# Two attention and gated-MLP layers in one kernel: key weights on GpSimd's queue, warm-ups on a cleared strip, new tables for the order

## The chip, the cores and the metric

The kernel runs on one core of a Trainium2 chip. The metric is the device time of one execution in microseconds, as the median of several runs. Times inside an execution come from one profiled execution, and are counted from its first instruction.

## The reference

The input `x` has 2048 rows of 512 numbers in bf16. Two layers with the same weights follow each other. Each layer adds two blocks to `x`, and each block works on the layer norm of `x`.

```python
def _A_ref(x, wqkv, wo):              # H = 32 heads of 16, window W = 256
    qkv = (x @ wqkv).reshape(B, S, 3, H, Dh)          # then to q, k, v by head
    scores = einsum("bhqd,bhkd->bhqk", q, k) * Dh ** -0.5
    mask = (i - j >= 0) & (i - j < W)                 # a causal sliding window
    p = softmax(where(mask, scores, -1e9))
    return einsum("bhqk,bhkd->bhqd", p, v).reshape(B, S, D) @ wo

def _B_ref(x, w_gate, w_up, w_down):  # F = 1792
    h = sigmoid(x @ w_gate) * (x @ w_up)
    return h @ w_down

for layer in range(2):
    x = x + _A_ref(layernorm(x), A_wqkv, A_wo)
    x = x + _B_ref(layernorm(x), B_w_gate, B_w_up, B_w_down)
```

## The kernel before

All weights and all of `x` stay in SBUF. The 2048 rows are 16 tiles of 128 rows; four tiles are a group, for which queries, keys and values are projected. `layer_norm` makes one tile's normalised rows: statistics on DVE (`stats`, L589 to L592), one over the root on POOL (`root`, L598 and L599), the scaling into `xn` on DVE (`apply`, L617), and then the transposed copy `xnT`. The first tiles are transposed by PE (L638) and copied out by ACT or DVE (L666, L668); the later ones go by a transposing DMA on SP's queue (L656), two tiles at a time.

PE's matmuls are the projections (queries L703, keys L734, values L770), the scores (L1029, L1040, L1050), the values times the probabilities (L1109), the output projection (L893), gate and up of the MLP (L798, called GLU in the code), and down (L862). Scores and values run with the array split, four small matmuls side by side; the others use it whole. ACT takes the exponential of a whole score buffer, `Sps`, at once (L1082, 128 x 2048 elements). One such step is a visit. There is one score buffer, so the next scores wait for the exponential ahead of them. A layer has 77 visits, the kernel 154. There are 64 blocks of values, two for each tile in each layer. After the values come a transposition, the normalisation and a second transposition (by PE for tiles 0 and 1, by SP's queue for the others), then the output projection, and after that the second layer norm, gate and up, and down.

`GLU` says how many tiles share one pass over gate and up: a pass over one, two or four tiles has matmuls of 128, 256 or 512 columns. A pass over four tiles can begin when `xnT` of all four is there. `TAIL` cuts the last tile's down product into 384 and 128 columns.

No order of instructions is written by hand. `Plan` is a small model of the chip that runs while the kernel is built. It keeps a clock for each engine, durations for each kind of work (such as `EXP_NS`, `SWITCH`, or the number that `scores` returns), and the times at which DMAs land. Whenever an engine is free in this model, the ready task with the lowest priority number is emitted on it; PE's next piece of work is chosen in `pick` and `choose`. So the order on every queue follows from the tables: `PRIO` and `LATE_PRIO` for the tasks of ACT, DVE, POOL and SP, `RANK` and `LATE_RANK` for PE, `SLACK` and `LATE_SLACK` for what is added to a DMA's landing, `OPT` for variants, and `PACE`. `PACE` holds the smallest time between the starts of two visits: entry 0 in layer 0, entry 1 in layer 1, entry 2 in the first 12 visits, entry 3 from there to visit 23. The LATE tables hold after visit 23. On the chip the order is fixed, and each engine waits by semaphores for what it needs.

Where the model has nothing for PE, `keep_warm` (L1292) emits four matmuls of 128 columns whose result nobody reads. Their operand is the identity `ident`, which POOL makes first thing in `constants`. POOL also writes `nhalf`, the exponent of `root`, and clears the halves of `Vl` and `Vh` (L534) that the copies from `Vaug` leave alone. `Vl` and `Vh` are filled by DMAs on SP's queue (L1314).

`loads` issues the inputs on the queues of SP and ACT: tiles 0 to 3 of `x` in halves, then the weights of the keys, of the queries (each in two transfers of 256 KB, one on each queue), and of the values, then the other inputs. `has_wq["k"]` is the event that a key projection waits for in the model.

Of the kernel before, what the change touches and what calls it, by code (L numbers as in the profile page):

```python
# [12 lines left out]
P = 128  # L13
# [43 lines left out]
def pool_ns(n):  # L57
# [2 lines left out]

EXP_NS = 1880
TAIL = (384, 128)
GLU = [[[1] * 4 + [4], [1] * 4 + [2] * 2, [1] * 6 + [2], [1] * 8, [2] * 4, [1] * 2 + [2] * 3, [2] * 2 + [4]], [[4] * 3 + [2, 1, 1], [4] * 3 + [2, 2], [4] * 4]]
PACE = [2682, 3207, 1600, 2511, 23.52]
EARLY = 12
FILL = 800
OVERLAP = {"ACT": 114, "DVE": 83, "POOL": 45, "SP": 0}
# [1 line left out]
EXTRA = {"ACT": 40, "DVE": 10, "POOL": 30, "SP": 0}  # L69
PE_LATENCY = 180  # L70
COLD = 5200
SWITCH = 96
LAND = 1230
RATE = ((3300, 330.0), (5300, 160.0), (1e9, 345.0))
FIRST = 1100
# [3 lines left out]
FETCH = (1200, 2300)  # L79


PRIO = dict(st_x0=7.13, ap_x0=2.72, xt_x0=3.36, st_x1=-0.44, ap_x1=1.86, xt_x1=6.58, st_x=18.87, ap_x=6.56,
    xt_x=2.0, st_p=7.13, ap_p=4.46, xt_p=0.81, st_g=2.23, ap_g=1.32, xt_g=6.14, st_g0=5.97, ap_g0=3.21,
    xt_g0=1.33, tp=5.75, tp_g=-0.06, q=4.0, q0=5.51, q1=4.74, k=1.95, k0=-0.89, k1=-1.49, s=-1.15, s0=5.46,
    s1=3.28, v=0.28, v0=5.43, v1=14.72, vv=5.53, exp=3.64, exp0=4.71, m0=4.61, m00=-0.56, e0=1.11, e00=1.28,
    e1=7.21, e10=6.56, m2=0.64, m20=3.6, th=5.12, mu=-0.12, dn=1.29, add=-0.27, add0=1.8, out=-2.4, mv=5.8,
    mv0=6.23, oq=-2.27, oq0=-0.14, no=4.71, no0=2.61, on=5.93, on0=0.59, vc=9.2, vc0=-0.87)
OPT = dict(gu='SP', g1=1, bk=3, bq=2, wide=0, r0=2, g0=1, g2=1, x0=1, eps=1, hold=0, own=1, ck=0, cq=2,
    turn=2)
SLACK = dict(xt=1208, oq=843, on=211, vc=1208)  # L90
RANK = dict(tp=-1.708, o=-2, lead=14.747, far=7.411, v=9.3, g=1.778, d=1.823, feed=11.672, x3=21097, wd=474,
    go=364)
LATE_PRIO = dict(st_p=-0.04, ap_p=7.96, xt_p=-0.99, st_x=1.07, ap_x=4.81, xt_x=-1.16, st_g=1.75, ap_g=1.19,
    xt_g=2.76, q=3.84, k=4.33, s=4.05, v=0.61, exp=1.12, m0=4.62, e0=2.79, e1=4.39, m2=5.49, th=1.65, mu=2.51,
    dn=2.1, add=0.69, out=0.45, mv=3.49, oq=0.77, no=6.44, on=2.16, vc=0.22)
LATE_SLACK = dict(xt=489, oq=1327, on=2346, vc=897)
LATE_RANK = dict(tp=-2, o=1.576, lead=9.722, far=6.159, v=1.796, g=1.769, d=3.896, feed=7.551, go=1418)

# [268 lines left out]
class Net:  # L369
# [74 lines left out]
    def loads(self, A_x, wqkv, wo, w_gate, w_up, w_down):  # L444
        nc, pl = self.nc, self.pl
        wq_src = wqkv.rearrange("(k p) m -> p k m", p=P)
        wo_src = wo.rearrange("(k p) m -> p k m", p=P)
        wd_src = w_down.rearrange("(c p) m -> p c m", p=P)
        wg_src = w_gate.rearrange("(k p) f -> p k f", p=P)
        wu_src = w_up.rearrange("(k p) f -> p k f", p=P)  # L450
        self.has_x, self.has_wq = {}, {}

        def load(dst, src, nbytes, after=0, prio=2, queue="SP", ns=650, row=2 * D):
            q = {"SP": nc.sync, "ACT": nc.scalar}[queue]
            return pl.dma(ns, nbytes, lambda: q.dma_start(out=dst, in_=src), (), prio, after, queue, bulk=(queue, row)).done

        def load_x(dst, tiles, n, prio=2, queues=("SP", "SP"), after=0):
            done, parts = Event(), []
            for z in range(2):
                src = A_x[0].rearrange("(t z k) d -> z k t d", z=2, k=HP)[z][:, tiles, :]  # L460
                parts.append(load(dst[z:P:2], src, n * HP * D * 2, after, prio, queues[z], 780))
            when_all(parts, done.fire)
            return done

        def x_group(g, after=0):
            h = slice(g * NBG, (g + 1) * NBG)
            ev = load_x(self.xsb[:, h, :], h, NBG, after=after)
            for t in range(g * NBG, (g + 1) * NBG):
                self.has_x[t] = ev

        def both(parts):
            done = Event()
            when_all(parts, done.fire)
            return done

        for t, n in {1: ((0, 1), (1, 1), (2, 2)), 2: ((0, 2), (2, 2)), 3: ((0, 1), (1, 3))}[OPT["x0"]]:
            ev = load_x(self.xsb[:, t:t + n, :], slice(t, t + n), n, 0, ("SP", "ACT"))
            for i in range(t, t + n):
                self.has_x[i] = ev
        if OPT["wide"]:  # L480
            self.has_wq["q"] = self.has_wq["k"] = both([
                load(self.wq[:, k:k + 2, 0:2 * D], wq_src[:, k:k + 2, 0:2 * D], 4 * P * D * 2, prio=0, queue=q, row=4 * D)
                for k, q in ((0, "ACT"), (2, "SP"))])
        else:
            for w in "kq":
                h = slice("qk".index(w) * D, ("qk".index(w) + 1) * D)
                self.has_wq[w] = both([load(self.wq[:, k:k + 2, h], wq_src[:, k:k + 2, h], 2 * P * D * 2, prio=0, queue=q)
                                       for k, q in ((0, "ACT"), (2, "SP"))])
        self.has_wq["v"] = load(self.wq[:, :, 2 * D:3 * D], wq_src[:, :, 2 * D:3 * D], D * D * 2, prio=0, queue="ACT")
        x_group(1)  # L490
        self.has_wo = load(self.wot[:], wo_src, D * D * 2)
        x_group(2)
        gu = [load(w[:, k:k + 2], src[:, k:k + 2], D * F, prio=0 if OPT["gu"] == "ACT" else 2, queue=OPT["gu"], row=2 * F)
              for w, src in ((self.wg, wg_src), (self.wu, wu_src)) for k in (0, 2)]
        self.has_gu = both(gu)
        at = RANK["x3"]
        x_group(3, at)
        parts = []
        for i in range(0, FC, 2):
            h = slice(i, i + 2)  # L500
            parts.append(load(self.wd[:, h, :], wd_src[:, h, :], 2 * P * D * 2, after=at + 2 * RANK["wd"] * i))
        self.has_wd = both(parts)

    def constants(self):
        nc = self.nc
        nc.gpsimd.memset(self.nhalf[:], -0.5)
        nc.gpsimd.memset(self.ident[:], 0.0)
        nc.gpsimd.affine_select(out=self.ident[:], in_=self.ident[:], compare_op=ALU.not_equal, fill=1.0,
                                base=0, pattern=[[-1, P]], channel_multiplier=1)
        for i in range(2):  # L510
            self.ones(i, nc.vector)
        nc.vector.memset(self.rms[0][:], 0.0)
        for m in range(4):
            nc.vector.memset(self.rms[0][32 * m:32 * m + 16, :], 1.0)
        nc.vector.tensor_scalar(out=self.rms[1][:], in0=self.rms[0][:], scalar1=-1.0, scalar2=1.0,
                                op0=ALU.mult, op1=ALU.add)
        for i in range(2):
            self.zeros(0, i)
        self.pl.free["POOL"] = 3000.0
        self.pl.free["SP"] = self.pl.free["ACT"] = 750.0  # L520
        self.pl.at(750.0)
        self.pl.at(1500.0)
        self.pl.free["DVE"] = 3600.0
        self.pl.at(3600.0)
# [11 lines left out]
    def later_constants(self):  # L536
        nc, pl = self.nc, self.pl
# [10 lines left out]
        def mask2(e):  # L548
            for z in range(2):
# [7 lines left out]
            nc.vector.tensor_scalar(out=self.maske[:, 1], in0=self.maske[:, 0], scalar1=-1.0, scalar2=1.0,  # L557
                                    op0=ALU.mult, op1=ALU.add)

        for i in range(2):  # L560
            self.vzero[i] = pl.task({"POOL": 800}, lambda e, i=i: self.zeros(1, i), first, prio=8, port=True).done
        for i in range(2, VP):
# [439 lines left out]
    def scores(self, L, t, kind, i):  # L1002
# [5 lines left out]
        if kind == "A":  # L1008
# [21 lines left out]
                                         rhs=self.qT[32 * m:32 * m + 32, i, q0:q0 + n * HP],  # L1030
                                         start=True, stop=True, tile_position=(32 * m, 0))
            runs = cut
            return pl.count(8 * len(runs)) or 220
        if kind == "R":
            zs = range(2 if t + 2 < NT else 1)
            for z in zs:
                for cq in range(NCQ):
                    q0, o = ((L * NT + t) * 2 + 5 * z) % (QG * TGW // HP) * HP, (z * NCQ + cq) * HP
                    for m in range(4):
# [1 line left out]
                                         lhsT=kTp[32 * m:32 * m + 32, cq, tt].rearrange("p e k -> p (e k)")[:, z:2 * P:2],  # L1041
                                         rhs=self.qT[32 * m:32 * m + 32, cq, q0:q0 + HP],
                                         start=True, stop=True, tile_position=(32 * m, 0))
            return pl.count(16 * len(zs)) or 122 * len(zs)
        for cq in range(NCQ):
            for e in range(2):
                o = (2 * cq + e) * HP
                q0 = ((L * NT + t) * 2 + 1) % (QG * TGW // HP) * HP
                for m in range(4):
                    nc.tensor.matmul(self.sps[:, m, o:o + HP], lhsT=kTp[32 * m:32 * m + 32, cq, tt, e, :],  # L1050
                                     rhs=self.qT[32 * m:32 * m + 32, cq, q0:q0 + HP],
                                     start=True, stop=True, tile_position=(32 * m, 0))
        return pl.count(32) or 230

    def exp(self, L, t, kind, i):
        nc = self.nc
# [27 lines left out]
    def values(self, L, t, half, bank):  # L1084
# [7 lines left out]
        for col in range(4):  # L1092
# [10 lines left out]
            for k, (where, Va, p) in enumerate(parts):  # L1103
# [6 lines left out]
                                     stop=k == len(parts) - 1 or t == 0, tile_position=(0, 32 * g))  # L1110
                n += 0.5 + 0.5 * (k == 0 and t > 0)
                pl.count(4)
        return n * 56

    def after_values(self, L, t, half, bank, done):
        nc, pl = self.nc, self.pl
# [171 lines left out]
    def keep_warm(self, bank):  # L1288

        nc, pl = self.nc, self.pl  # L1290
        for i in range(4):
            nc.tensor.matmul(self.banks[bank][:, 0:P], lhsT=self.ident[:], rhs=self.ident[:], start=True, stop=True)  # L1292
        pl.count(4)
        pl.matmul("d", 4 * 56)

# [7 lines left out]
    def half_values(self):  # L1303
# [18 lines left out]
        for z in range(2):  # L1322
            some = pairs if z == 0 else [k for k in pairs if k[1] + 2 < NT]
            for i, (L, t) in enumerate(some):
                V = self.Vaug[(L * NT + t) // 2 % VP]
                deps = [self.v_ready[L, t], self.v_ready[L, t + 1]]
                if z and i < 2:
                    deps.append(self.vzero[i])
                if i >= 2:
                    old = some[i - 2]  # L1330
                    deps += both(old[0], old[1] + 1 + 2 * z)
# [81 lines left out]
    def go(self, *srcs):  # L1413
# [26 lines left out]
        self.slot = 0  # L1440
        self.last_s = -1e9
        self.pv_list = [k + (h,) for k in LT for h in range(2)]
        self.constants()
        self.loads(*srcs)
        self.streams = [[], [], [], [], []]
        self.roots, self.pairs, self.vones, self.vzero = {}, {}, {}, {}
        self.applied = [Event() for _ in range(NBG)]
        for t in range(NBG):
            self.layer_norm(("p", 0, 0), t, [self.has_x[t]])
# [72 lines left out]
```

The softmax here doesn't subtract the row's maximum and nothing guards it: scores larger than these inputs give would overflow.

## Time and profile before

| what | value |
|---|---|
| median of 3 runs | 541.65 us (540.52 to 541.98) |
| span of the profiled execution | 539.6 us |
| PE busy | 531.1 us, 98% |
| DVE busy | 420.5 us, 78% |
| ACT busy | 382.3 us, 71% |
| POOL busy | 43.4 us, 8% |
| PE's first matmul starts, last one ends | 1.45 us, 536.35 us |
| first and last exponential start | 13.94 us, 471.26 us |
| warm-up matmuls | 64, all before 9.5 us |

No time of the profiled execution other than its span is given. PE's busy time counts from a matmul's start to its modelled end; neighbours overlap, so the mean duration of a row is longer than the distance between two starts. PEld is the loading of the stationary operand, beside the matmuls. The chain of work that ended last starts at the last instruction and goes back, at each step, to what released it.

### The profile page before, as it was taken

To read this page: it belongs to the slowest core of one execution; us is meant where nothing else is said; L and a number is where in the kernel's file an instruction comes from. 1 tells how busy PE (TensorE), PEld (TensorE's weight loads), DVE (VectorE), ACT (ScalarE), POOL (GpSimd) and SP (SyncE) were. 2 spreads that over 40 slices of the span, in tenths; PEclk is the share of its full clock that TensorE was granted. 3 is DMA by queue.
4 is the path that set the end of the run, shared out by engine and by line. 5 is a ranking of instruction groups with operands and counts; after the bars stand their busy time and mean duration, and the time that the engine had idled before them with its cause. 6 is when DMAs were issued, how large, how long until landed. Compare 5 with 4: busy or idle time off the path is not lost.

```text
span 539.6 us, 21359 instructions
## 1 busy us (share of the span) xinstructions
PE 531.1 (98%) x9658; PEld 293.0 (54%) x9658; DVE 420.5 (78%) x844; ACT 382.3 (71%) x380; POOL 43.4 (8%) x99
## 2 busy tenths in 40 slices
PE   8999999999999999999999999999999999999997
PEld 8446755855767444544444444544444444455873
DVE  6999999789878997798977789778677785674442
ACT  4989989878888687776778767787667866540330
POOL 5301110001000110101100010101000000000000
PEclk9999999999999999999999999999999999999999
DMA  8890334232421323143110622117211241132001
GB/s 260 317 227 15 43 72 57 50 61 63 72 52 33 72 51 60 36 101 59 32 35 14 105 51 47 38 42 108 54 45 28 60 72 50 24 70 58 2 11 39
DMA packets 95067, 36.23 MB, mean 67 GB/s; under 512 B 78336, under 2 KB 93952, under 8 KB 94976
## 3 DMA queue, kind: packets, MB, share of 16 engines
q1 hardware_dynamic: 93600, 33.56, 29.9%
q8 instruction: 75, 1.23, 1.0%
q10 hardware_dynamic: 1376, 1.31, 0.8%
q14 instruction: 16, 0.13, 0.1%
HBM read 9.70 MB, written 2.10 MB: 22 GB/s over the span
## 4 chain that ended last, share of the span: by engine, by line
PE 89%; DVE 5%; ACT 2%; DMA 1%; issue 1%; POOL 0%; SPq 0%; ACTq 0%; POOLq 0%
PE bank L798 37%; PE bank L862 18%; PE bank L1109 9%; PE Sps L1029 7%; PE bank L893 5%; PE bank L734 4%; PE bank L770 3%; PE bank L703 3%; PE Sps L1040 2%; ACT PTring L1082 1%; DMA wq<-in_A_wqkv_dram 1%; DVE kTp L749 1%; DVE st L589 1%; DVE PTring L960 1%; DVE edge L960 1%
## 5 line engine op out<-in xcount | busy, mean ns | idle before, releaser
L1082 ACT ACTIVATE PTring<-Sps 128x2048 bf16<-128x2048 f32 (+1 forms) x122 | 226.0, 1852 | 63.2 <-PE Sps L1029 59.2
L798 PE MATMUL bank<-xnT,wu 128*128 128x512 bf16 (+2 forms) x728 | 128.2, 297 | 0.0
L798 PE MATMUL bank<-xnT,wg 128*128 128x512 bf16 (+2 forms) x728 | 128.2, 298 | 0.0
L862 PE MATMUL bank<-wd,hT 128*128 128x512 bf16 (+2 forms) x462 | 109.9, 373 | 0.0
L824 DVE SCALAR_TENSOR_TENSOR hT<-hT,bank 128x256 bf16<-128x256 bf16 (+1 forms) x154 | 80.8, 537 | 34.0 <-ACT hT L816 21.2
L816 ACT ACTIVATE hT<-bank 128x256 bf16<-128x256 f32 (+1 forms) x154 | 71.1, 482 | 48.5 <-PE bank L798 47.8
L798 PEld LDWEIGHTS <-wg 128*128 128x128 bf16 x728 | 60.7, 98 | 36.7 <-issue 2.3
L798 PEld LDWEIGHTS <-wu 128*128 128x128 bf16 x728 | 61.4, 98 | 34.5 <-issue 2.5
L1082 ACT ACTIVATE edge<-Sps 128x2048 bf16<-128x2048 f32 (+1 forms) x32 | 56.6, 1770 | 17.3 <-PE Sps L1040 17.3
L862 PEld LDWEIGHTS <-hT 128*128 128x128 bf16 x462 | 43.0, 98 | 46.4 <-issue 2.2
L668 DVE CAST OTs<-bank 128x512 bf16<-128x512 f32 x59 | 43.0, 729 | 21.5 <-PE bank L1109 21.1
L960 DVE TENSOR_TENSOR PTring<-PTring,mask 128x1024 bf16<-128x1024 bf16 x64 | 43.7, 684 | 12.3 <-ACT PTring L1082 12.1
L1109 PE MATMUL bank<-PTring,Vaug 128*32 128x64 bf16 (+1 forms) x2880 | 52.0, 203 | 0.0
L1109 PEld LDWEIGHTS <-Vaug 128*32 128x32 bf16 x2880 | 44.0, 97 | 12.0 <-issue 10.4
L1029 PE MATMUL Sps<-qT,kTp 32*128 32x256 bf16 (+3 forms) x1216 | 47.4, 248 | 1.2 <-ACT PTring L1082 1.1
L598 POOL TENSOR_SCALAR st<-st 128x2 f32<-128x2 f32 (+1 forms) x33 | 10.7, 325 | 443.6 <-DVE st L590 443.6
L589 DVE BATCH_NORM_STATS2 st<-xsb 128x6 f32<-128x512 bf16 x64 | 43.9, 686 | 1.7 <-DMA xsb<-in_A_x_dram 1.2
L1109 PE MATMUL bank<-edge,Vl 128*32 128x64 bf16 x1024 | 44.4, 193 | 0.1
L960 DVE TENSOR_TENSOR edge<-edge,maske 128x1024 bf16<-128x1024 bf16 x60 | 40.3, 682 | 3.4 <-ACT edge L1082 3.3
L1029 PEld LDWEIGHTS <-kTp 32*128 32x128 bf16 x1216 | 18.2, 92 | 45.4 <-issue 43.5
L1109 PE MATMUL bank<-edge,Vh 128*32 128x64 bf16 x896 | 40.8, 193 | 0.0
L960 DVE TENSOR_TENSOR PTring<-PTring,maskn 128x1024 bf16<-128x1024 bf16 x56 | 38.2, 682 | 0.0
(73 smaller groups left out, 522.0 us busy)
## 6 DMA issues: line engine op xcount, KB each, us to landing
Vl<-Vaug SPq DMA_DIRECT2D x32, 68.0 KB, 2.4
out_dram<-xsb SPq DMA_DIRECT2D x15, 128.0 KB, 2.1
Vh<-Vaug SPq DMA_DIRECT2D x28, 68.0 KB, 2.5
wg<-in_B_w_gate_dram SPq DMA_DIRECT2D x2, 896.0 KB, 9.7
wu<-in_B_w_up_dram SPq DMA_DIRECT2D x2, 896.0 KB
wd<-in_B_w_down_dram SPq DMA_DIRECT2D x7, 256.0 KB, 5.3
xsb<-in_A_x_dram SPq DMA_DIRECT2D x6, 256.0 KB, 7.4
wq<-in_A_wqkv_dram ACTq DMA_DIRECT2D x2, 256.0 KB, 4.5
```

The lines of the kernel that those rows point to most:

```text
L589: nc.vector.bn_stats(out=st[:, 0:6], in_=self.xsb[:, t, :])
L668: self.nc.vector.tensor_copy(out=out, in_=in_)
L734: return [(mm_ns(w), lambda kt=kt, o=o: nc.tensor.matmul(self.banks[bank][:, o:o + w], lhsT=self.wq[:, kt, D + cq * P:D + cq * P + P], rhs ...
L798: return [(mm_ns(w), lambda i=i, j=j, fc=fc, wt=wt, kt=kt: self.nc.tensor.matmul(pt[:, i, j, :], lhsT=wt[:, kt, fc * P:(fc + 1) * P], rhs= ...
L816: self.nc.scalar.activation(out=self.hT[:, ch[0] * GW:ch[0] * GW + size], in_=pt, func=AF.Tanh, scale=0.5)
L824: self.nc.vector.scalar_tensor_tensor(out=h, in0=h, scalar=1.0, in1=pt, op0=ALU.add, op1=ALU.mult)
L862: nc.tensor.matmul(self.banks[bank][:, 0:w], lhsT=self.hT[:, at:at + P], rhs=self.wd[:, fc, d], start=fc == 0, stop=fc == FC - 1)
L893: return [(mm_ns(D), lambda c=c: nc.tensor.matmul(self.banks[bank][:], lhsT=b[0][:, c, :], rhs=self.wot[:, c, :], start=c == 0, stop=c == ...
L960: done = pl.task({"DVE": dve_bf_ns(1024)}, lambda e: nc.vector.tensor_tensor(out=r, in0=r, in1=m.to_broadcast([P, 16, HP]), op=ALU.mult), ...
L1029: nc.tensor.matmul(self.sps[:, m, o:o + n * HP], lhsT=kTp[32 * m:32 * m + 32, i, tt, e, :], rhs=self.qT[32 * m:32 * m + 32, i, q0:q0 + n * ...
L1082: nc.scalar.activation(out=out, in_=src, func=AF.Exp, scale=scale)
L1109: nc.tensor.matmul(o, lhsT=Va[:, c0:c0 + 32], rhs=p(h), start=k == 0 or t == 0, stop=k == len(parts) - 1 or t == 0, tile_position=(0, 32 * g))
```

## The change

The key weights' two transfers leave the queues of SP and ACT and are issued on GpSimd's queue, ahead of all of POOL's memsets. In the model their arrival is the constant `KEYS_NS`. The clearing of the `Vl` halves moves from `constants` to tasks (`lzero`) that are released by the root of tile 3, and the copies into `Vl` wait for it. The warm-up matmuls read the first 128 columns of `hT`, which DVE clears first thing, in place of `ident`. `hT` is otherwise the buffer of gate times up, and is first written for that much later. Several costs of the model are set higher: `SWITCH`, the scores (220 to 234, 122 to 126, 230 to 244) and the values (56 to 59.3). All tables get new numbers; `hold=1` lets the statistics of tiles 2 and 3 wait for the scaling of the tile two before, and `r1` is read nowhere. Layer 0's first half is cut into single tiles and pairs in another order; layer 1 goes from three groups of 4 tiles and two pairs to four groups of 4.

```diff
-GLU = [[[1] * 4 + [4], [1] * 4 + [2] * 2, ...], [[4] * 3 + [2, 1, 1], [4] * 3 + [2, 2], [4] * 4]]
-PACE = [2682, 3207, 1600, 2511, 23.52]
+GLU = [[..., [1, 1, 2, 1, 1, 2], [1, 1, 1, 1, 2, 2]], [[4, 4, 4, 4], [4, 4, 4, 4], [4, 4, 4, 4]]]
+PACE = [2682, 3226.51, 1293.37, 0, 23.52]
...
-SWITCH = 96
+KEYS_NS = 6600
+SWITCH = 100
...
-OPT = dict(gu='SP', g1=1, bk=3, bq=2, wide=0, r0=2, g0=1, g2=1, x0=1, eps=1, hold=0, own=1, ck=0, cq=2,
-    turn=2)
-SLACK = dict(xt=1208, oq=843, on=211, vc=1208)
+OPT = dict(gu='SP', g1=1, bk=3, bq=2, wide=0, r0=2, g0=5, g2=1, x0=1, eps=1, hold=1, own=1, ck=0, cq=2,
+    turn=2, r1=1)
+SLACK = dict(xt=3684, oq=1183, on=0, vc=1448)
...
-            for w in "kq":
+            for w in "q":
...
-    def constants(self):
+    def constants(self, wqkv):
         nc = self.nc
+        nc.vector.memset(self.hT[:, 0:P], 0.0)
+        src = wqkv.rearrange("(k p) m -> p k m", p=P)
+        for k in (0, 2):
+            nc.gpsimd.dma_start(out=self.wq[:, k:k + 2, D:2 * D], in_=src[:, k:k + 2, D:2 * D])
+        self.has_wq = {"k": Event()}
+        self.pl.at(KEYS_NS, self.has_wq["k"].fire)
         nc.gpsimd.memset(self.nhalf[:], -0.5)
...
-        for i in range(2):
-            self.zeros(0, i)
-        self.pl.free["POOL"] = 3000.0
+        self.pl.free["POOL"] = 3700.0
...
+        for i in range(2):
+            self.lzero[i] = pl.task({"POOL": 800}, lambda e, i=i: self.zeros(0, i), first, prio=5.5, port=True).done
...
-            return pl.count(8 * len(runs)) or 220
+            return pl.count(8 * len(runs)) or 234
...
-        return n * 56
+        return n * 59.3
...
-            nc.tensor.matmul(self.banks[bank][:, 0:P], lhsT=self.ident[:], rhs=self.ident[:], start=True, stop=True)
+            nc.tensor.matmul(self.banks[bank][:, 0:P], lhsT=self.hT[:, 0:P], rhs=self.hT[:, 0:P], start=True, stop=True)
...
-                if z and i < 2:
-                    deps.append(self.vzero[i])
+                if i < 2:
+                    deps.append((self.lzero, self.vzero)[z][i])
```

The other tables (`PRIO`, `RANK`, `LATE_PRIO`, `LATE_SLACK`, `LATE_RANK`) change in nearly every number.

More of the change, by code (lines that the diff above doesn't have):

```diff
@@ L62 @@
 TAIL = (384, 128)
-GLU = [[[1] * 4 + [4], [1] * 4 + [2] * 2, [1] * 6 + [2], [1] * 8, [2] * 4, [1] * 2 + [2] * 3, [2] * 2 + [4]], [[4] * 3 + [2, 1, 1], [4] * 3 + [2, 2], [4] * 4]]
-PACE = [2682, 3207, 1600, 2511, 23.52]
+GLU = [[[1, 1, 2, 1, 1, 2], [1, 1, 1, 1, 2, 2], [1, 1, 1, 1, 1, 1, 2], [1, 1, 2, 1, 1, 2], [2, 2, 2, 2], [1, 1, 2, 1, 1, 2], [1, 1, 1, 1, 2, 2]], [[4, 4, 4, 4], [4, 4, 4, 4], [4, 4, 4, 4]]]
+PACE = [2682, 3226.51, 1293.37, 0, 23.52]
 EARLY = 12
@@ L79 @@
 FETCH = (1200, 2300)
[L82 to L87, printed above, removed]
@@ L88 @@
-OPT = dict(gu='SP', g1=1, bk=3, bq=2, wide=0, r0=2, g0=1, g2=1, x0=1, eps=1, hold=0, own=1, ck=0, cq=2,
-    turn=2)
-SLACK = dict(xt=1208, oq=843, on=211, vc=1208)
[L91 to L95, printed above, removed]
@@ L96 @@
-LATE_SLACK = dict(xt=489, oq=1327, on=2346, vc=897)
-LATE_RANK = dict(tp=-2, o=1.576, lead=9.722, far=6.159, v=1.796, g=1.769, d=3.896, feed=7.551, go=1418)
+PRIO = dict(st_x0=5.517, ap_x0=3.263, xt_x0=-2.449, st_x1=0.535, ap_x1=2.037, xt_x1=-0.264, st_x=21.878,
+    ap_x=6.56, xt_x=0.304, st_p=6.13, ap_p=4.803, xt_p=1.447, st_g=3.212, ap_g=3.753, xt_g=8.638,
+    st_g0=5.969, ap_g0=10.645, xt_g0=1.805, tp=6.151, tp_g=-5.567, q=2.826, q0=5.911, q1=4.398, k=1.523,
+    k0=-1.653, k1=-0.168, s=0.884, s0=5.29, s1=3.157, v=0.602, v0=2.264, v1=12.226, vv=5.994, exp=1.727,
+    exp0=3.904, m0=4.754, m00=-0.127, e0=0.225, e00=0.363, e1=7.302, e10=6.163, m2=0.812, m20=4.348,
+    th=9.414, mu=-0.12, dn=1.29, add=6.967, add0=0.098, out=-5.025, mv=10.502, mv0=3.452, oq=-3.44,
+    oq0=-1.409, no=4.71, no0=2.789, on=6.342, on0=7.39, vc=9.458, vc0=-3.8)
@@ new lines @@
+OPT = dict(gu='SP', g1=1, bk=3, bq=2, wide=0, r0=2, g0=5, g2=1, x0=1, eps=1, hold=1, own=1, ck=0, cq=2,
+    turn=2, r1=1)
+SLACK = dict(xt=3684, oq=1183, on=0, vc=1448)
+RANK = dict(tp=-7.096, o=-19.273, lead=11.363, far=3.245, v=4.087, g=0.973, d=13.876, feed=10.496,
+    x3=36461.883, wd=540.461, go=54.04)
+LATE_PRIO = dict(st_p=4.477, ap_p=6.912, xt_p=-19.42, st_x=11.351, ap_x=-0.429, xt_x=-5.57, st_g=0.885,
+    ap_g=-1.483, xt_g=0.152, q=2.406, k=2.254, s=-6.511, v=-1.275, exp=-0.273, m0=4.508, e0=0.951,
+    e1=4.685, m2=2.787, th=-3.045, mu=0.343, dn=2.495, add=-3.89, out=6.413, mv=3.344, oq=-0.04, no=5.156,
+    on=3.828, vc=12.682)
@@ L101 @@
+LATE_SLACK = dict(xt=214, oq=824, on=3443, vc=382)
+LATE_RANK = dict(tp=3.166, o=-19.355, lead=7.503, far=19.11, v=0.482, g=4.796, d=14.138, feed=-3.568,
+    go=915.623)
 class Late(dict):
@@ L450, in loads @@
         wu_src = w_up.rearrange("(k p) f -> p k f", p=P)
-        self.has_x, self.has_wq = {}, {}
+        self.has_x = {}
         def load(dst, src, nbytes, after=0, prio=2, queue="SP", ns=650, row=2 * D):
@@ L1043, in scores @@
                                          start=True, stop=True, tile_position=(32 * m, 0))
-            return pl.count(16 * len(zs)) or 122 * len(zs)
+            return pl.count(16 * len(zs)) or 126 * len(zs)
         for cq in range(NCQ):
@@ L1052, in scores @@
                                      start=True, stop=True, tile_position=(32 * m, 0))
-        return pl.count(32) or 230
+        return pl.count(32) or 244
     def exp(self, L, t, kind, i):
@@ L1442, in go @@
         self.pv_list = [k + (h,) for k in LT for h in range(2)]
-        self.constants()
+        self.constants(srcs[1])
         self.loads(*srcs)
         self.streams = [[], [], [], [], []]
-        self.roots, self.pairs, self.vones, self.vzero = {}, {}, {}, {}
+        self.roots, self.pairs, self.vones, self.vzero, self.lzero = {}, {}, {}, {}, {}
         self.applied = [Event() for _ in range(NBG)]
```

## The prediction

> **What bounds the kernel now.** I read the page first, then the busy time by stretch, then PE's waits, then the chain for the first microseconds, then the timeline at the end. The page:
>
> ```profile
> span 539.6 us, 21359 instructions
> PE 531.1 (98%) x9658; PEld 293.0 (54%) x9658; DVE 420.5 (78%) x844; ACT 382.3 (71%) x380; POOL 43.4 (8%) x99
> ...
> PE   8999999999999999999999999999999999999997
> ...
> ACT  4989989878888687776778767787667866540330
> ```
>
> PE is busy 98% of the span, in every slice but the first and last. A busy PE need not be a useful one, so I took the distances between matmul starts in the timeline. Behind a 512-column matmul the next starts after 216 ns, behind 256 columns after 109 ns, behind 128 after 56 ns, nearly everywhere: PE streams. The same stretches by window:
>
> ```profile
> 0.00:10.00 10.00, 7.86 (x95) 7.67 (x95) 6.33 (x29) 2.60 (x4) 5.72 (x23) 1.00 0.73 228
> ...
> 20.00:30.00 10.00, 9.30 (x127) 4.07 (x126) 9.63 (x23) 9.23 (x12) 2.94 (x6) 1.00 0.76 247
> ...
> 170.00:300.00 130.00, 129.94 (x2337) 61.33 (x2336) 109.54 (x208) 97.73 (x88) 10.49 (x18) 1.00 0.25 51
> 300.00:480.00 180.00, 180.00 (x3342) 85.49 (x3341) 136.54 (x249) 127.80 (x112) 9.05 (x16) 1.00 0.30 56
> ```
>
> (Length, then PE, PEld, DVE, ACT and POOL busy, clock, DMA share, GB/s.) From 170 us on PE is never free. From 10 to 40 us DVE, ACT and PE are all over 90%: there the order matters. Adding up every distance between starts that exceeds the median of its kind by over 30 ns gives 0.86 + 0.24 us in 7.6 to 14 us, 2.10 in 14 to 40, 1.04 in 40 to 100, 1.69 in 100 to 171, and nothing later. So 4.83 us after 14 us is all that a better order could still win from stalls. PE's own list of waits shows the piece that the keys have in it:
>
> ```profile
> PE bank L1292 <- POOL ident L508: 1.4, 1, 1.4
> PE Sps L1029 <- ACT PTring L1082: 1.1, 4, 0.4
> PE bank L734 <- DMA wq<-in_A_wqkv_dram: 0.7, 1, 0.7
> ```
>
> The chain that ended last, in the first 20 us, goes through the same transfer:
>
> ```profile
> 3.02 5.51 DMA wq<-in_A_wqkv_dram
> 8.54 0.05 issue
> 8.58 0.73 PE bank L734 x10
> 9.31 0.22 PE bank L1292 x4
> ```
>
> The half of the key weights on SP's queue is issued at 3.02 us and lands at 8.54. PE had begun the keys of tile 0 at 7.62, did two matmuls, stood 0.86 us, then did the other ten and four warm-ups (0.22 us).
>
> **What the Trainium skill says.** "DMA: Bandwidth & Descriptors", Issuing engines are not separate DMA queues: transfers from SP, ACT and GpSimd run on the same 16 DMA engines, so another issuer saves issue time only. The windows agree as far as they go: 260 GB/s in 4 to 6 us and 308 in 6 to 7 with two issuers; none shows three. "SBUF — State Buffer", A bandwidth-pool intuition that's wrong, with the box ahead of it: a DVE instruction in a two-port mode keeps GpSimd from writing descriptors. No trace of before shows a GpSimd DMA; DVE does memsets from 1.07 to 2.1 us. "TensorE: Matmul & The Clock Gate", Part 1: full clock comes after some 3.4 us of sustained work. Here warm-ups start at 1.45, are 107 ns apart until 6.0 and 56 from 6.5 on, so it took longer. "TensorEngine Tiling (Array Packing)", Key Properties: a change of tiling drains PE. The trace agrees: 512 columns ahead of a score matmul take 312 ns and not 216, so a crossing costs 96 ns; I count 377.
>
> **Part by part**, against the profiled execution's span of 539.6 us. The page gives no other time of that execution; the median of the runs, 541.65, is 2.05 above it, and I carry that over.
>
> *Keys on POOL.* SP and ACT each lose one issue (0.64 and 0.61 us), so queries, values, later x tiles, wo and the GLU weights are issued that much earlier. POOL gains two issues ahead of nhalf, ident and the square roots. When do the keys land? x tiles 0 to 3 and the keys together are 1.05 MB. At the rates of before, 2 to 4 us moves 370 KB, 4 to 6 us 520 and 6 to 7 us 308, so 1.05 MB is through near 6.5 us, plus landing: **6.7 us**. The skill's price (Anatomy of one DMA) of 2.0 us plus bytes/436e3, 2.6 us for 256 KB, is below that as an estimate. Bounds: 6.0 us, and 8.5 if descriptors or sharing cost as much as they save. xnT of tile 0 is written at 7.29, so at 6.7 keys no longer hold anything. The 0.86 us stall and the four warm-ups in front of real work go: 1.08. But tile 1's xnT is done only at 8.41 and queries landed at 8.7 and 9.97, with total bytes unchanged, so some fill returns. I take **-0.8 us**; from -1.6 (tile 2's transposes also move, from 9.43 towards xn's end at 8.40) to +1.5 (late keys, or x tiles delayed by the third queue).
>
> *What waits behind POOL's issues.* ident must be there for tile 0's transposes at 6.12 and nhalf for the first root at 4.53. POOL is free from 2.94 to 4.41 and gives up six memsets of Vl there (1.61 us), about two issues' worth. At SP's 0.6 us an issue this costs nothing: 0.78 + 1.2 + 0.61 for nhalf and ident ends at 2.6. From 1.55 us an issue on it ends past 4.5, and the roots follow one for one: 0, up to +1.
>
> *Memsets and strip.* The Vl memsets return as tasks behind tile 3's root (8.81 us). With the masks and ones of Vaug the queue then is some 1.6 us longer; first readers are Vl copies at 21.21 and the values of Vaug 2 to 4 after that: 0, and without that cover up to 1.6 on roots of tiles 4 on (15.03). The strip of hT costs DVE one memset near 0.1 us, with DVE idle from 2.10 to 3.28. Warm-ups then start some 0.2 us earlier; they wait for DVE and no longer for ident. 0, from -0.3 (clock up earlier) to +0.1.
>
> *Tables.* Only the order changes, not the matmuls, with two exceptions. Layer 1's last groups go from 4,4,4,2,2 tiles to 4 times 4: 224 matmuls of 256 columns at 109 ns become 112 of 512 at 216, 24.42 against 24.19: **-0.2**. Layer 0's first half keeps four single tiles and two pairs, in another order: 0. Crossings: 154 visits make at least 308, and 64 value blocks 64 more if each directly follows scores; that is 372 against 377: at best -0.5, I take **-0.2**, up to +1. The stalls of 4.83 us: the tables were laid anew against longer assumed costs for scores and values, which can place work better or merely elsewhere. No row shows it. Bounds -3.8 and +4; I take **-1.5**, a choice, since DVE, ACT and PE stay full from 10 to 40 us.
>
> *The end.* The last group of four can now start only with tile 15:
>
> ```profile
> 495.13 1.42 SPq L656 DMA_TRANSPOSE xnT<-xn  x1
> ...
> 497.02 0.60 PE L798 MATMUL bank<-xnT,wg 128*128 128x256 bf16 x4
> ```
>
> That transpose lands at 498.39 in the trace. Behind it then lie 24.2 us of gate and up, 12.1 of down (56 x 216 ns) and 3.2 from PE's last matmul to the end of the span: 537.9. Before, tiles 12 and 13 ran first, so this did not bind; the slack was 1.7 us. With 2.7 us taken off the rest (0.8 + 1.5 + 0.2 + 0.2) the end would be 536.9, and it does bind. Where the landing goes: earlier scores -0.9 (tile 2's transposes), no pace in visits 12 to 23 at most -0.9 (period 2.51 us to some 2.43, the 1.88 of an exp and 0.55 for the scores behind it), layer 1's pace 19.5 ns x 77 = +1.5. That is -0.3, hence 537.6; an earlier phase that gains a little more brings it between. I take **+0.3**.
>
> Sum: -0.8 - 0.2 - 0.2 - 1.5 + 0.3 = -2.4, span 537.2, time **539.2 us**.
>
> **Rivals.**
> 1. *The last group waits (slower).* If tile 15's transposes land later than 501.7 us, the same 39.5 us behind them give a span over 541.2 and a time over 543.3. For it: pace adds 1.5, so early visits that lose 1.8 us are enough, and 10 to 40 us has no free engine. Against: visits 12 to 23 lose their pace. With landing at 502.5, 544.1 us.
> 2. *Stall moves only.* Keys land, but queries (9.97) or xnT hold PE; new stalls replace old. Only -0.2 to -0.8 remains: 541.1. For it: same bytes on the same DMA engines.
> 3. *Nearly all goes.* -0.8 - 3.8 - 0.5 - 0.2 with tile 15 early enough: 536.4. Against: it needs the landing 3 us earlier.
> 4. *The GpSimd load does not bring keys forward*: landing at 8.5, first part 0, tables alone: 540.0.
>
> **How the numbers follow.** A measurement here tells 0.3%, 1.6 us, from no change: faster is below 540.0, slower above 543.3. My forecast and rival 3 hold 0.55 (0.43 and 0.12), and lie mostly below 540.0. Rivals 2 and 4 hold 0.22 (0.16 and 0.06), within. Rival 1 holds 0.23. The range leaves out the best part of rival 3 and the worst of rival 1: 535.8 to 544.2. The forecast's own range is 537.5 to 540.5.
>
> **What would show it.** Right: wq for the keys landing before 7 us; no wait of PE on wq ahead of tile 0's ten matmuls; first exp before 13.2 us (13.94 now); stalls after 14 us near 3.3 us; PE full from 170 us on, with no gap ahead of the last group's first 512-column gate. Wrong: a gap near 497 us with PE waiting for xnT (rival 1); ident or a root late on POOL after 4.5 us; stalls between 14 and 171 us at 5 us or more (rival 2).

## The result, and the profile after

The changed kernel takes 545.28 us in the median (544.61 to 545.49), against 541.65 before: a ratio of 1.0067, with a 95% interval of 1.0055 to 1.0079. It is slower by 3.6 us, where 2.4 us less was forecast, and outside the range given. The profiled execution took 544.61 us.

The page of after, first the span and the engines' busy time, then the DMA queues that carry the inputs (packets, megabytes, share of the engines):

```profile
span 542.9 us, 21126 instructions
...
PE 530.9 (98%) x9542; PEld 281.7 (52%) x9542; DVE 416.3 (77%) x829; ACT 382.1 (70%) x368; POOL 45.5 (8%) x101
...
q1 hardware_dynamic: 93328, 33.29, 30.3%
...
q10 hardware_dynamic: 1104, 1.05, 0.6%
q0 software_dynamic: 160, 0.52, 0.3%
```

PE is as busy as before in a longer span. The last line is the key weights on GpSimd's queue. By stretch (columns as in the prediction):

```profile
0.00:10.00 10.00, 6.85 (x83) 6.46 (x83) 5.57 (x26) 2.46 (x3) 4.33 (x13) 1.00 0.76 245
...
20.00:30.00 10.00, 8.81 (x121) 4.25 (x121) 9.83 (x24) 9.05 (x12) 2.53 (x7) 1.00 0.56 177
...
170.00:300.00 130.00, 129.24 (x2367) 62.54 (x2367) 107.23 (x205) 100.01 (x91) 9.59 (x16) 1.00 0.29 52
300.00:480.00 180.00, 179.72 (x3353) 85.35 (x3352) 137.13 (x253) 128.49 (x113) 9.11 (x16) 1.00 0.31 58
480.00:524.00 44.00, 44.00 (x206) 19.95 (x204) 18.51 (x31) 10.75 (x18) 0.93 (x2) 1.00 0.08 19
```

PE loses a microsecond in the first ten (6.85 busy for 7.86), half of one from 20 to 30, and it is no longer full from 170 us on. Its waits:

```profile
PE Sps L648 <- DVE xn L627: 2.1, 2, 1.3
PE Sps L1039 <- ACT PTring L1092: 1.3, 3, 0.6
PE bank L808 <- DMA xnT<-xn: 1.1, 2, 0.7
PE bank L1302 <- DVE hT L510: 1.0, 1, 1.0
PE bank L648 <- DVE Vaug L678: 1.0, 1, 1.0
```

The wait on the keys is gone, as forecast. In its place PE waits 2.1 us for the normalised rows (`xn`) of the first tiles. The chain in the first microseconds no longer goes through `wq`:

```profile
2.32 5.11 DMA xsb<-in_A_x_dram
7.45 0.70 DVE st L599
```

To see where the 3.3 us of the span come in, I laid the traces of both kernels side by side by amount of PE work: at each time in before, how much later after has done as much (each matmul counted with its streaming time, from the starts of the weight loads).

| time in before, us | 10 | 40 | 60 | 80 | 171 | 210 | 400 | 533 |
|---|---|---|---|---|---|---|---|---|
| after is late by, us | 0.6 | 1.2 | 1.1 | 1.9 | 2.1 | 2.8 | 3.7 | 3.5 |

About 0.6 us are lost at the start, and the rest in pieces spread over the whole kernel. (From 14 to 40 us the figure swings between 0.1 and 1.2 us, because the two orders place the same work differently there.)

### The profile page after: what moved, and what is told of

It is laid out like the page before. It is cut to its first block, busy times and chain, and to the rows that moved or that the text cites. A ratio compares the mean times of both kernels' runs of the same rounds, so it can differ in the third digit from the quotient of the medians.

```text
span 542.9 us, 21126 instructions
## 1 busy us (share of the span) xinstructions
PE 530.9 (98%) x9542; PEld 281.7 (52%) x9542; DVE 416.3 (77%) x829; ACT 382.1 (70%) x368; POOL 45.5 (8%) x101
## 3 DMA queue, kind: packets, MB, share of 16 engines
q10 hardware_dynamic: 1104, 1.05, 0.6%
## 4 chain that ended last, share of the span: by engine, by line
PE 85%; DVE 8%; DMA 3%; ACT 2%; issue 1%; POOL 1%; ACTq 0%; DVEq 0%
PE bank L808 35%; PE bank L872 16%; PE bank L1119 8%; PE Sps L1039 6%; PE bank L903 5%; PE bank L713 4%; PE bank L780 4%; PE bank L744 3%; PE Sps L1050 2%; ACT PTring L1092 2%; DMA xnT<-xn 2%; DVE PTring L970 1%; DMA xsb<-in_A_x_dram 1%; DVE st L599 1%; DVE kTp L759 1%
## 5 line engine op out<-in xcount | busy, mean ns | idle before, releaser
L808 PE MATMUL bank<-xnT,wg 128*128 128x512 bf16 (+2 forms) x672 | 125.7, 308 | 1.5 <-DMA xnT<-xn 1.1
L808 PE MATMUL bank<-xnT,wu 128*128 128x512 bf16 (+2 forms) x672 | 126.4, 308 | 0.0
L834 DVE SCALAR_TENSOR_TENSOR hT<-hT,bank 128x512 bf16<-128x512 bf16 (+1 forms) x140 | 78.8, 576 | 43.9 <-PE bank L808 31.7
L872 PE MATMUL bank<-wd,hT 128*128 128x512 bf16 (+2 forms) x462 | 107.9, 373 | 0.0
L826 ACT ACTIVATE hT<-bank 128x512 bf16<-128x512 f32 (+1 forms) x140 | 69.1, 511 | 52.2 <-PE bank L808 50.8
L808 PEld LDWEIGHTS <-wg 128*128 128x128 bf16 x672 | 55.6, 98 | 43.1 <-issue 3.5
L808 PEld LDWEIGHTS <-wu 128*128 128x128 bf16 x672 | 55.9, 98 | 40.0 <-issue 2.5
L678 DVE CAST OTs<-bank 128x512 bf16<-128x512 f32 x54 | 39.4, 730 | 20.1 <-PE bank L1119 19.3
```

The source lines that it names most:

```text
L678: self.nc.vector.tensor_copy(out=out, in_=in_)
L808: return [(mm_ns(w), lambda i=i, j=j, fc=fc, wt=wt, kt=kt: self.nc.tensor.matmul(pt[:, i, j, :], lhsT=wt[:, kt, fc * P:(fc + 1) * P], rhs= ...
L826: self.nc.scalar.activation(out=self.hT[:, ch[0] * GW:ch[0] * GW + size], in_=pt, func=AF.Tanh, scale=0.5)
L834: self.nc.vector.scalar_tensor_tensor(out=h, in0=h, scalar=1.0, in1=pt, op0=ALU.add, op1=ALU.mult)
L872: nc.tensor.matmul(self.banks[bank][:, 0:w], lhsT=self.hT[:, at:at + P], rhs=self.wd[:, fc, d], start=fc == 0, stop=fc == FC - 1)
```

## The experiments

Three questions: does the keys' new queue cost the time, do the tables, and if the tables, which? Ratios are to runs of before on the same chip, with 95% intervals.

**The queue with the order held.** In these four kernels the model still plans as in its parent, and PE's order is the parent's. The key transfers are issued elsewhere, and b_keys and b_latekeys also take over the warm-ups on the cleared strip of `hT`, which was not exchanged alone. The cuts show the lines that move the transfer.

```diff
# b_keys: before, with the strip of hT; in constants, ahead of nhalf (nothing emitted for them in loads)
+        for k in (0, 2):
+            nc.gpsimd.dma_start(out=self.wq[:, k:k + 2, D:2 * D], in_=src[:, k:k + 2, D:2 * D])
# b_latekeys: the same two lines behind the Vl memsets
# a_hwkeys: after without these two lines; in loads, ahead of each query transfer
+                    q.dma_start(out=self.wq[:, keys:keys + 2, D:2 * D], in_=wq_src[:, keys:keys + 2, D:2 * D])
# a_latekeys: after, Vl memsets back in constants, the two lines behind them
```

b_keys: 

> The order of before on every queue, with the key weights issued by GpSimd as its first work, nhalf, ident and the Vl memsets behind them, and warm-ups on the cleared strip of hT. Theory A (the keys on the third queue crowd out the x tiles): keys land near 5.1 and 6.3 us, the ACT half of x tiles 2 and 3 lands near 7.4 instead of 5.5 or so, the first exponential starts near 15.2 us instead of 13.94, time 542.7 to 543.2. Theory B (the queue is harmless, the new order costs all of the 3.6 us): first exponential at 13.0 to 14.0, time 540.9 to 541.7.

b_latekeys: 

> As b_keys, but GpSimd issues the keys behind nhalf, ident and the Vl memsets, near 3.0 us and not 1.3. Theory A: the x tiles land as in before (all four by 5.6 us), keys by 7.5 us, PE's wait on the keys is gone, first exponential 13.0 to 13.9, time 540.8 to 541.6. Theory B: within 0.4 us of b_keys.

a_hwkeys: 

> The order of after on every queue, with the key weights on the queues of ACT and SP, right ahead of the query weights, as in before; none on GpSimd. Theory A: x tiles all landed by 5.6 us, first exponential 13.5 to 14.2 us instead of 15.27, time 543.6 to 544.2 (about 1.4 less than after). Theory B: 545.0 to 545.5, since the order is that of after.

a_latekeys: 

> The order of after, with GpSimd's memsets of nhalf, ident and the Vl halves first and the keys behind them, near 3.0 us. Theory A: x tiles landed by 5.8 us, keys by 7.5 us, first exponential 13.3 to 14.2, time 543.5 to 544.2. Theory B: 545.0 to 545.5.

| order of | keys on ACT and SP | keys first on POOL | keys late on POOL |
|---|---|---|---|
| before | 541.65 | 541.72; 1.0011 (1.0003 to 1.0019) | 545.17; 1.0067 (1.0049 to 1.0085) |
| after | 544.17; 1.0053 (1.0041 to 1.0065) | 545.28; 1.0067 (1.0055 to 1.0079) | 546.19; 1.0085 (1.0072 to 1.0098) |

The queue costs 0.6 us in the order of before (by the ratio; 0.2 to 1.0 by its interval). In the order of after it is 0.8 us by the ratios and 1.1 by the medians, but there the two intervals overlap. The kernel after without any key weight on POOL (a_hwkeys) still takes 2.9 us more than before. So theory A has the mechanism at the start right and its size too high: the first exponential of b_keys starts at 14.50 us and not at 15.2. Theory B names the larger part. The time of a_hwkeys is in theory A's range, though its first exponential starts at 14.81 us and not by 14.2. The two kernels with late keys lie outside both theories.

The mechanism is seen at DVE's statistics, which start when an x tile has landed. From the timeline of before, then of after, b_keys and a_hwkeys, the second and third tile:

```profile
4.30 0.70 DVE L589 BATCH_NORM_STATS2 st<-xsb 128x6 f32<-128x512 bf16 x1
...
5.64 0.69 DVE L589 BATCH_NORM_STATS2 st<-xsb 128x6 f32<-128x512 bf16 x1
```
```profile
5.32 0.69 DVE L599 BATCH_NORM_STATS2 st<-xsb 128x6 f32<-128x512 bf16 x1 [0.96 <-DMA xsb<-in_A_x_dram]
...
7.45 0.69 DVE L599 BATCH_NORM_STATS2 st<-xsb 128x6 f32<-128x512 bf16 x1 [0.70 <-DMA xsb<-in_A_x_dram]
```
```profile
5.59 0.69 DVE L593 BATCH_NORM_STATS2 st<-xsb 128x6 f32<-128x512 bf16 x1 [1.25 <-DMA xsb<-in_A_x_dram]
...
6.92 0.69 DVE L593 BATCH_NORM_STATS2 st<-xsb 128x6 f32<-128x512 bf16 x1
```
```profile
4.29 0.69 DVE L602 BATCH_NORM_STATS2 st<-xsb 128x6 f32<-128x512 bf16 x1
...
5.63 0.69 DVE L602 BATCH_NORM_STATS2 st<-xsb 128x6 f32<-128x512 bf16 x1
```

With keys on GpSimd, DVE waits for x; without, it does not. The second tile is 1.0 to 1.3 us late, and all that follows with it. The first tile is held too, because DVE scales it only after the statistics of the second: at 6.60 us in b_keys and 6.34 in after, for 5.32 in before. (In b_keys the first root on POOL is late as well, 5.24 us for 4.53, but it ends at 5.82, ahead of that scaling.) The packets say how: between 3.0 and 5.5 us the trace of after has 484 KB on GpSimd's queue and 249 KB on SP's and ACT's together, where before had 582 KB on those two. A GpSimd packet is 3.3 KB on average (0.52 MB in 160), one of ACT's 0.95 KB. That the larger packet is what wins the larger share fits, but no run varies the packet size, so it stays a guess.

Late keys show the other side. In b_latekeys the x tiles land as before (statistics of tile 1 at 4.28), but the two key transfers, issued at 2.90 and 3.81 us, land at 8.45 and 11.28, and PE waits. After the wait its granted clock (third number from the end) is at half for a while:

```profile
PE bank L738 <- DMA wq<-in_A_wqkv_dram: 3.5, 2, 2.5
```
```profile
12.00:14.00 2.00, 2.00 (x22) 2.00 (x20) 0.11 (x1) 0.43 (x1) 0.00 (x0) 0.50 1.11 359
```

I had expected 7.5 us for the keys. Issued first, the keys displace x; issued later, they land later than they did from SP and ACT. The 3.6 us of b_latekeys are not the wait alone: its two executions with a mean clock of 1.0 took 543.33 and 543.76 us, the four at 0.993 to 0.997 took 544.92 to 547.01. How much of the difference is the clock's was not taken apart.

**Tables exchanged.** The tables in force up to visit 23 and those after it can be exchanged apart.

```diff
# b_early: before with PRIO, OPT, SLACK, RANK, the two early paces and layer 0's cut of after
# b_late: before with
-LATE_SLACK = dict(xt=489, oq=1327, on=2346, vc=897)
+LATE_SLACK = dict(xt=214, oq=824, on=3443, vc=382)
#   and LATE_PRIO, LATE_RANK, the paces of the two layers and layer 1's cut of after
# b_costs: before with
-SWITCH = 96
+SWITCH = 100
#   and after's costs of scores and values
# a_early: after with the late tables, late paces and layer 1's cut of before
# a_early_hw: the same on a_hwkeys
```

b_early: 

> The kernel before (keys on ACT and SP, warm-ups on ident) with only the tables that hold up to visit 23 taken from after: PRIO, OPT, SLACK, RANK, entries 2 and 3 of PACE, and the cut of layer 0's first half. Theory A (the early tables fit a start that the chip does not have, and lose there): first exponential at 14.3 to 15.0 us, twelfth near 47, time 542.6 to 544.0. Theory B (the late tables lose, by PE waiting for transposes): 541.0 to 541.8.

b_late: 

> The kernel before with only the tables of the time after visit 23 taken from after: LATE_PRIO, LATE_SLACK, LATE_RANK, entries 0 and 1 of PACE, and layer 1 in four groups of 4 tiles. Up to visit 23 its order is that of before. Theory A: 541.0 to 541.8 us, with at most 0.5 us of waits on PE after 171 us. Theory B: PE waits for xnT by a transposing DMA (LATE_SLACK xt 214 for 489), 1 to 2 us in all after 171 us, time 542.5 to 543.8.

b_costs: 

> The kernel before with only the model's higher costs (SWITCH 100, scores 234, 126 and 244, values 59.3) and its own tables. A new order follows from the same tables. If tables are worth something only with the costs that they were found for: 542.5 to 545 us. If longer costs are simply truer: 540.5 to 541.6. If an order of this kind is worth about the same whatever moves it: within 0.3 us of before.

a_early: 

> The kernel after (keys on GpSimd) with the tables of the time after visit 23, entries 0 and 1 of PACE and the cut of layer 1 taken from before. Up to visit 23 its order is that of after. If the losses of the late tables (PE waiting for xnT near 206 and 338 us) are theirs, they go: 543.9 to 544.7. If they only follow from the worse start, or the early order is all that loses: 545.0 to 546.

a_early_hw: 

> As a_early, with the keys on ACT and SP ahead of the queries, and none on GpSimd: the early order of after alone, in its own model. If early order, late order and keys add up (keys 1.1, late 0.7 to 1.0, early 1.5 to 2.0 of the 3.7 to 3.9): 543.0 to 543.6. If the early order costs nothing by itself: 541.3 to 542.

| kernel | median, us | ratio |
|---|---|---|
| b_early | 549.57 | 1.0148 (1.0129 to 1.0167) |
| b_late | 542.01 | 1.0014 (1.0007 to 1.0020) |
| b_costs | 546.04 | 1.0095 (1.0078 to 1.0112) |
| a_early | 545.44 | 1.0080 (1.0064 to 1.0095) |
| a_early_hw | 544.66 | 1.0063 (1.0051 to 1.0075) |

Of these five forecasts only a_early's second one (545.0 to 546) holds. b_late falls between its two; the other three are slower than anything that was expected.

a_early_hw is the early order of after, in its own model, with the late tables of before and no key weight on POOL: it already takes 3.4 us more than before by its ratio. Putting in the late tables of after (a_hwkeys, 1.0053) costs nothing further, and the keys on POOL bring the rest. So most of the loss belongs to what the early tables and the new costs lay down together. It does not all fall in the early stretch: by amount of PE work a_early_hw is 1.6 us late at 80 us, 1.1 at 171 and 3.7 at the end. More than half is lost after 171 us, under the late tables of before laid out with the new costs. The late tables taken alone (b_late) cost 0.8 us, with the wait that theory B named:

```profile
PE bank L800 <- DMA xnT<-xn: 1.0, 2, 0.5
```

But a_early, without those late tables, is no better than after: its median is 545.44, and the lowest of both is 544.6. (Its executions go up to 547.30; part of that is the clock at the start, as the last section shows.) The wait for `xnT` is real (after loses 0.8 us between 171 and 210 us, with one such wait of 0.7), yet giving up the tables that bring it does not win the time back. Halves of the change cost more than the whole: b_early 8 us, b_costs 5. In b_early, PE stands at 92 to 96 us, mostly behind one exponential (a wait of 2.0 us). The windows show what follows:

```profile
92.00:94.00 2.00, 1.12 (x91) 0.93 (x81) 1.54 (x4) 1.98 (x3) 1.43 (x2) 1.00 0.06 10
94.00:96.00 2.00, 0.41 (x16) 0.23 (x16) 1.69 (x4) 2.00 (x3) 0.14 (x1) 0.69 0.03 8
96.00:98.00 2.00, 1.51 (x72) 1.10 (x74) 1.29 (x2) 1.29 (x2) 0.00 (x0) 0.50 0.73 134
98.00:100.00 2.00, 2.00 (x44) 1.47 (x33) 0.73 (x1) 1.02 (x1) 0.00 (x0) 0.50 0.40 90
```

PE is idle for some 2.5 of 4 us and the granted clock falls to half for the next microseconds. The gap with its echo costs about 6 us between 80 and 100 us.

**Orders nudged.** Is an order from these tables stable at all?

```diff
# b_nudge1: before        # b_nudge2: before        # a_nudge: after
-SWITCH = 96              -EXP_NS = 1880            -SWITCH = 100
+SWITCH = 97              +EXP_NS = 1884            +SWITCH = 101
# a_pace: after
-PACE = [2682, 3226.51, 1293.37, 0, 23.52]
+PACE = [2682, 3226.51, 1293.37, 2511, 23.52]
```

b_nudge1: 

> The kernel before with the model's SWITCH at 97 and not 96; a change that means nothing by itself, after which the whole order is laid anew from the same tables. If tables and costs are fitted to each other as one (theory C): 542.5 to 547 us, with new waits on PE between 14 and 171 us. If an order from these tables is robust, and the early tables of after are simply worse: 540.9 to 541.9.

b_nudge2: 

> The kernel before with the model's EXP_NS at 1884 and not 1880. Theory C: 542.5 to 547 us, by another amount than b_nudge1. Robust order: 540.9 to 541.9.

a_nudge: 

> The kernel after with the model's SWITCH at 101 and not 100. Theory C: the tables of after are fitted to 100, so 546 to 549 us. If after is not a fitted point for the chip, only an ordinary order: 543.5 to 547 either way, as likely below after as above it.

a_pace: 

> The kernel after with PACE entry 3 at 2511 as before, so that visits 12 to 23 are held apart again; up to visit 11 the order is that of after. If the missing pace is what costs PE 0.8 us between 60 and 80 us: 544.2 to 544.8. If a new order from visit 12 on is what counts (theory C): 546 to 549.

b_nudge1 is no test: its order is that of before but for a few matmuls, and its time is 541.30, ratio 0.9999 (0.9989 to 1.0010). b_nudge2 has a new order from some 20 us on: 542.97, ratio 1.0029 (1.0019 to 1.0039), 1.6 us more by the ratio. It loses 3 us between 40 and 50 us, as b_costs does there, and wins part of it back. That is within the forecast of theory C. a_nudge is 543.74, ratio 1.0039 (1.0027 to 1.0051), about 1.5 us *less* than after, against theory C. But by the names in the trace its order differs from that of after only between 35 and 53 us. Its profiled execution is 0.8 us shorter than after's; 0.3 of that is there at 10 us, before the orders part, and 0.4 comes between 171 and 210 us, where its wait for `xnT` is shorter. So the gain is measured, but that it comes from the order is not shown. What holds is this: a change of one cost by 0.2 to 1% can leave the order alone, or move the time by some 1.5 us, and after is not a point at which its tables and costs fit this chip best.

a_pace, 546.23 and 1.0083 (1.0068 to 1.0097), falls in theory C's range, with executions from 544.15 to 547.00. By amount of PE work it is 0.6 us behind after at 10 us, where both have the same order, and no less behind at 60 and 80: in the stretch from 60 to 80 us the pace gives nothing back, so the missing pace is not the cause there. What comes later is another matter. At 171 us a_pace is 0.6 us ahead of after, and at 210 it is over 2 us behind: PE waits 2.2 us for one exponential, and the clock averages 0.83 from 190 to 200 us. Its total therefore says little about the pace.

**Can the start be better?**

```diff
# b_split: before, keys 384 KB on ACT and 128 KB on SP, queries 128 KB and 384 KB
+                ks = {("k", "ACT"): slice(0, 3), ("k", "SP"): slice(3, 4), ("q", "ACT"): slice(0, 1), ("q", "SP"): slice(1, 4)}[w, queue]
# b_best: b_split with layer 1 in four groups of 4
# b_halfkeys: b_keys with only the k = 2 transfer on POOL, the k = 0 one on ACT as before
```

b_split: 

> The kernel before, in its own order, with the keys' two transfers cut 384 KB on ACT and 128 KB on SP, and the queries' 128 KB on ACT and 384 KB on SP, so that the keys are complete sooner without a third queue. If PE's wait of 0.86 us for the keys is worth its length: keys by 7.5 us, first exponential 13.0 to 13.6, time 540.4 to 541.0. If the wait is only passed on (queries, tile 2): 541.2 to 541.8.

b_best: 

> The kernel b_split (order of before, keys 384 KB on ACT and 128 KB on SP) with layer 1 cut in four groups of 4 tiles and no other table changed. If the merged last group saves the 0.2 us of its longer matmuls and is not held by tile 15's transposes (landing 498.4, which by the prediction allows an end of span at 537.9): 540.6 to 541.0. If it is held: 541.5 or more, with PE waiting for xnT near 497 us.

b_halfkeys: 

> The kernel b_keys with only the half of the keys that was on SP's queue (256 KB) on GpSimd as its first work; the other half stays on ACT behind x. If bytes of keys that run ahead push the x tiles back, half the bytes push them about half as far: statistics of tile 1 at 4.7 to 5.1 us (4.30 before, 5.59 in b_keys), first exponential 13.7 to 14.3, time 541.0 to 541.7. If a GpSimd transfer of any size holds the x tiles: as b_keys, 5.5 us and more.

b_split removes the wait for keys, its first exponential starts at 13.32 us for 13.94, and its time is 541.10, ratio 0.9996 (0.9990 to 1.0003): nothing that can be told from before. By amount of PE work it is ahead by 0.6 us until 100 us and level from 150 us on: the head start is gone by then. b_best, 541.40 and 0.9999 (0.9991 to 1.0007), adds nothing that shows; in its profiled execution PE waits 1.1 us for the query weights instead. b_halfkeys, 542.06 and 1.0019 (1.0009 to 1.0030), misses: with half the bytes the statistics of tile 1 start at 5.30, nearly as late as with all. The delay does not go by the bytes of the whole transfer. The first microsecond of it, 3.0 to 4.0 us, suggests why. In b_halfkeys the queues were, in packets, megabytes and share of the engines (q0 is GpSimd's, q1 SP's, q10 ACT's):

```profile
q0 software_dynamic: 50, 0.19, 90.2%
q10 hardware_dynamic: 41, 0.03, 9.2%
q1 hardware_dynamic: 9, 0.01, 2.6%
```

In b_keys it is 0.14 MB on GpSimd's queue and 0.03 on the other two, in before 0.21 on those two. In that microsecond the queues that carry x hardly move, and half the keys are enough for that. No version beat before.

## Why the prediction was wrong

By its own steps:

- *Arrival of the keys.* Forecast 6.7 us; they landed at 5.11 and 6.34, and PE's wait on them went. The figure is near, but not by the reckoning behind it, which let the keys come in behind the x tiles at the old rates. They came ahead of part of x, and 4 to 6 us moved 347 GB/s for 260.
- *Its worth, -0.8.* This step failed. The bound of +1.5 named the cause, x tiles delayed by the third queue, but I took the value from the side of the gain. x tiles 1 and 2 were 1.0 and 1.8 us later on DVE, the first exponential started at 15.27 us, and the queue cost 0.6 us in the order of before and, less surely, 0.8 to 1.1 in that of after. I had computed that 1.05 MB are through at 6.5 us, and that the keys would be among them. I had not asked which bytes come last: the x tiles did. The third issuer did more here than save issue time: it changed whose bytes moved. b_split adds that even without the harm the wait was worth under 0.6 us.
- *POOL's issues and memsets, 0.* Right. The issues took 0.92 and 0.74 us; ident was ready at 3.60 and the first root started at 4.45 (4.53 before). The Vl memsets returned at 11.57 us and no wait of PE or DVE is put down to them.
- *Matmuls merged and crossings, -0.2 and -0.2.* The trace has 0.22 us less of streaming and 376 crossings for 377. About right, too small to measure alone.
- *Stalls, -1.5.* The step that failed most. Counted as in the prediction, the stalls after 14 us went from 4.83 to 6.82 us, and PE's one crossing from values into scores takes a further 0.8. So the term was +2 to +3 and not -1.5. I called the value a choice, with bounds of -3.8 and +4. The choice rested on the new costs being longer and hence perhaps truer. a_early_hw shows the early tables with the new costs 3.4 us slower without the queue and without the new late tables; b_costs shows the same costs 5 us slower under the old tables.
- *The end, +0.3.* The last group's first gate came at 500.56, behind a transposition issued at 493.93, with PE full since 480 us:

```profile
493.93 1.23 SPq L666 DMA_TRANSPOSE xnT<-xn  x1
...
500.56 1.03 PE L808 MATMUL bank<-xnT,wg 128*128 128x512 bf16 x4
```

The rest being late, nothing waited there. Rival 1, my only case on the slower side, did not happen. The outcome is on its side by another mechanism: rival 2's moved stalls, with more new ones than old.

The chances carried the same error. PE at 98% busy and full from 170 us on left 4.8 us to win and no limit on what a different order may lose. That asymmetry was in the windows that I showed, and it spoke for slower.

What stays open: why the early order of after loses where it does. Of the pieces, the one at 19 us (a transposition waiting 1.0 us for DVE's copy of `Vaug`) is in a_hwkeys too, so it is the order's; about 1 us (0.8 to 1.2) between 60 and 80 us is in all five kernels with that early order, and no single wait there accounts for it. Why a_early_hw and a_hwkeys lose some 2 us more after 100 us, with either set of late tables, is open as well. The new costs and the early tables were never separated without a still larger loss (b_early, b_costs), so their shares are not known.

## What to carry to other kernels

When a transfer is sent ahead on a further queue, list what lands later for it, with the reader of each, before counting the gain. Where the bound engine is full, a new order has little to win and much to lose: price it by what a small change of the same tables does, here up to 1.6 us, and by the loss when tables and costs are not changed together, here up to 8. Compare orders with the transfer held, and transfers with the order held, and make sure that an order has changed before reading a time as its price.

## What the runs showed of the hardware

A GpSimd transfer of 256 KB took 0.92 and 0.74 us of POOL to issue, and 3.8 and 4.1 us from issue to landing when first (after); issued 1.6 us later it took 5.5 and 7.5 (b_latekeys). PE need not be idle for long for its clock to fall. In a_early's profiled execution, PE was busy about half the time from 4 to 8 us (1.09 and 0.98 of 2 us), and the clock then stayed at half until 14 us, though PE was full again from 10 us on:

```profile
6.00:8.00 2.00, 0.98 (x13) 0.99 (x14) 0.89 (x4) 0.55 (x1) 0.66 (x1) 0.87 0.94 301
8.00:10.00 2.00, 1.27 (x14) 1.00 (x12) 1.72 (x5) 0.04 (x1) 0.61 (x1) 0.50 1.05 371
10.00:12.00 2.00, 2.00 (x21) 2.00 (x20) 1.49 (x7) 0.58 (x1) 1.24 (x5) 0.50 1.11 358
```

The same order does not always bring this about. PE's order in after is that of a_early up to some 100 us, and in its profiled execution PE was busy 1.20 and 1.17 of 2 us from 6 to 10 us with the clock at 1.00. By amount of PE work the two executions are 1.9 us apart at 10 us.
